# A list scheduler's DMA times, its queue limit and its table of priorities are replaced in an attention and mixture-of-experts kernel

## The chip, the cores and the metric

The kernel runs on one core of one Trainium2 chip. The metric is the device time of one execution in microseconds (us). The core has five instruction streams that run side by side and meet at semaphores: PE (matrix multiply; its weight loads are shown as PEld), DVE, ACT, POOL, and SP, which here only issues DMAs. Each stream runs strictly in the order in which the program was written.

## What is computed

Attention in two resolutions makes x, and a mixture of eight experts is applied to x. Shapes: q, k, v are 4 x 8 x 576 x 64 (batch, head, position, width), x is 2304 x 512, w1 is 8 x 512 x 1024, w2 is 8 x 1024 x 512, all float32.

```python
q_d, k_d, v_d = (z.reshape(B, H, S // 4, 4, D).mean(axis=3) for z in (q, k, v))
out_up = np.repeat(sm_attn(q_d, k_d, v_d), 4, axis=2)          # coarse attention, full softmax
mask = np.abs(pos[:, None] - pos[None, :]) < 4
out_local = softmax(where(mask, scale * q @ k.T, -1e9)) @ v    # local attention, a band of 7
x = (out_up + out_local).transpose(0, 2, 1, 3).reshape(B * S, H * D)

noisy_logits = x @ w_gate + log1p(exp(x @ w_noise)) * noise
top2 = np.argpartition(-noisy_logits, 2, axis=1)[:, :2]        # and softmax weights over the two
for e in range(8):
    for k in range(2):
        mask = top2[:, k] == e
        out[mask] += top2_w[mask, k, None] * (relu(x[mask] @ w1[e]) @ w2[e])
```

## The kernel before

**Stages.** The first part computes attention, the routing, and the first layer of expert 0. The second part (the loop over e at the end) is a fixed sequence of matrix products: for each expert the second layer (`gemm2`, tiles py, L1195) of five tiles of 126 rows, and the first layer of the next expert (`gemm1`, tiles ph, L1170). The first part has no written order: a list scheduler makes it.

**Attention.** For each batch, `t_load` brings nine blocks of q and k (tiles nat, L416 and L419), `t_pe` transposes them on PE (pt, L427), `t_copy` and `t_sum`/`t_sumq` write the transposed copies and the sums over four positions (sq and qd, on POOL and DVE). `vd_load` brings v for the coarse attention (vg, L465), `vd_sum` and `vd_sum2` add it up on POOL (vh, vd). The `d_` steps are the coarse attention: scores sd, maximum, exponential, norm pd, transpose ptd, product od, spread up. The `l_` steps are the local attention over 20 tiles of 116 positions: `l_load_v` (vw, L587), scores sc, softmax sb, transpose ptl, product o (L647), the sum `l_x` into xT. A finished chunk of 128 rows is transposed (ptx), stored to DRAM (`l_store`, x_d, L688) and multiplied with the gate weights (`l_lg` to `l_ls`, tiles pl and ps).

**Routing.** The 18 chunks form five groups of 4, 4, 4, 2 and 4. For each group, ACT and DVE find the two experts of each row, PE counts positions (`r_pos`, tiles pp, L756 to L759), DVE computes slots (sli), and POOL writes one list entry per row and choice by indirect DMAs (`r_put`, list_d, L824), 36 in all, eight for a group of four chunks. After the third group, SP loads the list of expert 0 (`a_list`, L979), and POOL gathers three tiles of x rows for it (`b_gather`, gx, L993). The other two tiles of expert 0 take their rows from a product on PE (`b_list`, pb, L788) after the last group. Gathered tiles are copied (xr), transposed (ptg, L1097) and split; then `b_gemm` computes the first layer of expert 0 in two parts, ph0a (columns of the three tiles) and ph0b (the other two), both at L1117, eight steps f each.

**Other transfers.** `fetch_w1` loads eight blocks of expert 0's w1 (raw, L189), which ACT and DVE split into a high and a low part (w0h, w0l); `fetch_w2` the same for w2 (L192, w1h, w1l). `fill_out` writes zeros to the output in six DMAs of 768 KB (out_dram<-zero, L173). `fill_list` fills the lists.

**The scheduler.** Each piece of work is a `Step` with an engine, an assumed duration, the steps it needs, the buffers it takes from rings and frees, and a priority: a number that follows its batch, tile or chunk, plus an offset for its kind from the table `OFF`. `run_steps` takes, again and again, the step that can start first by the assumed times (with `SLACK` as tolerance, ties by priority) and emits it. A step of SP has a second number, `move`, the time for which its transfer occupies the one DMA queue that the scheduler knows; `free["move"]` is when that queue is free, and a transfer counts as landed 0.9 after its move. The scheduler's clock is only used while the program is built; on the chip the order stays, the times do not.

**Fillers.** Where the scheduler expects PE to be idle, `keep_warm` puts matmuls on a tile of ones (L364), whose result nobody reads.

The calls that make the steps of the first part are in the body of `tile_attn_moe_kernel`, with `move` and the duration as arguments. Two lines of `run_steps` set what an SP step costs:

```python
free["move"] = max(x.end + 0.5, free.get("move", 0.0)) + x.move
x.done = free["move"] + 0.9
```

Of the kernel before, what the change touches and what calls it, by code (L numbers as in the profile page):

```python
# [22 lines left out]
def kernel(  # L23
# [42 lines left out]
    NA = NTA * TR  # L66
    NBC = max(256, NCOL - NA)
# [24 lines left out]
    masks = []  # L92
# [175 lines left out]
    free = {}  # L268

    def run_steps(stage):  # L270

        todo = [x for x in steps if x.end is None and x.stage <= stage]
        while not all((not x.early, x.light, False)[stage - 1] for x in todo):
# [39 lines left out]
        "a_count": 19.6, "a_holes": 29.2, "a_list": -59.7, "a_rows": -6.7, "b_gather": -36.7,  # L313
        "b_gemm": -33.7, "b_hi": -59.3, "b_list": -39.3, "b_lo": 6.8, "b_order": -53.9, "b_pe": -51.4,
        "b_relu": 19.1, "b_rest": 19.4, "b_rows": -39.1, "b_weights": -39.8, "c_count": -47.8,
        "c_fills": 6.3, "c_first": -28.0, "c_ids": 24.7, "c_masks": 32.3, "c_route": -8.3, "c_sel": 14.0,
        "c_tiles": -19.3, "d_exp": -46.9, "d_max": -48.9, "d_norm": 4.3, "d_pt": -37.6, "d_ptc": -53.4,
        "d_pv": -51.1, "d_qk": -52.0, "d_rz": -58.3, "d_up": -21.6, "fetch_w1": 13.7, "fetch_w2": 22.7,
        "fill_list": -51.7, "fill_out": 36.3, "gather": -54.0, "identb": -47.2, "init_kz": -2.2,
        "l_exp": -29.6, "l_lg": -37.8, "l_lgc": -60, "l_lgt": -58.9, "l_load_v": 9.9, "l_ls": -52.8,  # L320
        "l_max": 18.0, "l_norm": 12.6, "l_pt": 6.9, "l_ptc": -12.8, "l_pv": 21.6, "l_qk": 31.9,
        "l_store": 24.9, "l_sum": 31.1, "l_x": -5.2, "l_xt": -23.7, "l_xtc": -17.5, "list_rows": -54.6,
        "load_list": -4.8, "load_noise": -32.5, "load_wgn": 14.3, "masks": -26.6, "ones": 19.0,
        "r_count": 38.4, "r_hot": -20.5, "r_oh": 31.7, "r_pay": -59.0, "r_pos": -33.2, "r_put": 33.4,
        "r_slot": 15.0, "r_soft": 23.3, "r_top": -38.1, "r_wexp": -4.9, "r_where": -60, "split_hi1": 40,
        "split_hi2": 31.3, "split_lo1": 26.2, "split_lo2": 32.3, "t_copy": -16.9, "t_load": -38.3,
        "t_new": 20.1, "t_pe": 6.3, "t_sum": -10.2, "t_sumq": 2.4, "vd_load": -27.3, "vd_sum": 0.9,
        "vd_sum2": -46.2, "warm": -38.1}
    SLACK = 0.15
# [28 lines left out]
    pw, warm = [], []  # L358
# [26 lines left out]
    KW = 0  # L385
# [17 lines left out]
    s_wgn = [Step("load_wgn", "sp", 0.65, lambda i=i: load_wgn(i), after=[s_fills], prio=KW + 0.5 * i, move=0.3) for i in range(2)]  # L403
    s_noise = [Step("load_noise", "sp", 0.5, load_noise, prio=KO, move=0.7)]
    s_fill = Step("fill_list", "sp", 0.45, fill_list, after=[s_fills], prio=2, move=0.5)
# [440 lines left out]
    for b in range(B):  # L846
# [42 lines left out]
        for u in range(5):  # L889
# [6 lines left out]
            a1 = Step("d_qk", "pe", 0.5 if u else 0.65, lambda b=b, u=u: d_qk(b, u), cols=576 if u else 2304, after=s_sum, use=[qdb], new=scb + [pdb], prio=pc_)  # L896
# [21 lines left out]
        for i in range(NB):  # L918
# [7 lines left out]
            a1 = Step("l_qk", "pe", 1.26, lambda n=n: l_qk(n), cols=4600, after=need + [s_masks], use=[qtb, kzb[b]], new=[scb], prio=n + KQ)  # L926
# [6 lines left out]
            a8 = Step("l_pv", "pe", 1.24, lambda n=n: l_pv(n), cols=2048, after=[a7, lv], use=[pTb, vwb], new=[ob], prio=n + KP)  # L933
# [6 lines left out]
            for ck, g, c, w in ps_:  # L940
# [6 lines left out]
                s_store += [Step("l_store", "sp", 0.45, lambda n=ck: l_store(n), after=[a11], use=[xb], move=0.7, **kw)]  # L947
                a12 = Step("l_lg", "pe", 0.3, lambda n=ck: l_lg(n), cols=2048, after=[s_x, s_sel] + s_wgn, use=[xTb[ck]], new=[lgb, lsb], **kw)
# [49 lines left out]
    for g, (n0, ni) in enumerate(groups):  # L998
# [213 lines left out]
    for part in range(2):  # L1212
        w_ = (NBC if part else NA) / 2400.0
# [160 lines left out]
```

## Time and profile before

| | us |
|---|---|
| median of 3 runs (lowest, highest) | 662.92 (661.96, 671.3) |
| the profiled execution | 662.21 |
| its span, first to last instruction | 660.5 |
| PE busy | 614.6 |
| DVE, ACT, POOL busy | 348.0, 259.9, 345.3 |
| first layer of expert 0 starts on PE | 202.77 |
| second layer of expert 0 starts on PE | 231.50 |

A row of a timeline gives start and duration in us, the engine, the line, the operation with output<-input, the shapes and the count; the bracket gives the idle time of the engine ahead of it and what ended that. SPq is the instruction stream of SP. A matmul's end is modelled, so PE's busy time counts fillers and slow matmuls alike. The granted clock is the share of full speed that PE was allowed.

### The profile page before, as it was taken

The numbers are of one execution on the slowest core, as the hardware profiler recorded it, in microseconds if no ns is written. First come the engines' busy times: TensorE is split into PE (matmuls) and PEld (weight loads), VectorE is DVE, ScalarE is ACT, GpSimd is POOL, SyncE is SP. The second block draws the span as 40 slices with busy tenths as digits, with TensorE's granted clock in tenths as the row PEclk, the third lists the DMA queues.
The fourth block names the chain that finished last, engine by engine and source line by source line (L and its number), as shares of the span: only waits on it lengthen the run. The fifth ranks groups of instructions, "written<-read, shape, count | busy, mean of one in ns | idle before, by whom it ended". The sixth has DMA issues, their size and how long they took to land.

```text
span 660.5 us, 12445 instructions
## 1 busy us (share of the span) xinstructions
PE 614.6 (93%) x4710; PEld 539.1 (82%) x4710; DVE 348.0 (53%) x784; ACT 259.9 (39%) x530; POOL 345.3 (52%) x415
## 2 busy tenths in 40 slices
PE   8878697888989999999999999999999999999993
PEld 6566586666879988988998998899899889889982
DVE  5557486676966445355345435544543544453310
ACT  6658585945643332332233233233323323322200
POOL 6464334678457563746556374464656527553011
PEclk9789797979989999999999999999999999999997
DMA  9889897742355334635534463563554436455111
GB/s 170 166 185 286 200 220 173 180 117 68 108 135 99 95 106 147 176 114 169 161 111 146 131 179 107 152 174 92 170 159 139 132 115 184 123 166 142 34 45 33
DMA packets 139354, 92.66 MB, mean 140 GB/s; under 512 B 74624, under 2 KB 121216, under 8 KB 139284
## 3 DMA queue, kind: packets, MB, share of 16 engines
q1 hardware_dynamic: 126052, 62.75, 37.0%
q0 software_dynamic: 13232, 29.02, 15.5%
q8 instruction: 39, 0.64, 0.4%
q14 instruction: 31, 0.25, 0.1%
HBM read 72.66 MB, written 19.95 MB: 140 GB/s over the span
## 4 chain that ended last, share of the span: by engine, by line
PE 79%; DMA 8%; DVE 3%; POOL 3%; issue 2%; SPq 1%; ACT 1%; POOLq 0%; DVEq 0%; ACTq 0%
PE py L1195 34%; PE ph L1170 30%; PE ph0a L1117 3%; DMA nat<-in_q_dram 2%; PE sc L599 2%; PE ph0b L1117 2%; DMA nat<-in_k_dram 2%; PE pt L427 2%; DMA gx<-x_d,cl 1%; PE o L647 1%; PE ptd L540 1%; DMA raw<-in_moe_w_dram 1%; POOL list_d L824 1%; PE sd L503 1%; DMA vg<-in_v_dram 1%
## 5 line engine op out<-in xcount | busy, mean ns | idle before, releaser
L1070 POOL DMA_INDIRECT gx<-x_d,gi x140 | 143.4, 1024 | 50.3 <-issue 48.4
L1170 PE MATMUL ph<-xh,w0h 128*128 128x316 f32 x448 | 137.8, 308 | 0.0
L1170 PE MATMUL ph<-xl,w0h 128*128 128x316 f32 x448 | 137.8, 307 | 0.0
L1170 PE MATMUL ph<-xh,w0l 128*128 128x316 f32 x448 | 137.7, 307 | 0.0
L1195 PE MATMUL py<-w1l,hh 128*126 128x512 f32 x320 | 126.2, 394 | 0.0
L1195 PE MATMUL py<-w1h,hh 128*126 128x512 f32 x320 | 126.2, 394 | 0.0
L1195 PE MATMUL py<-w1h,hl 128*126 128x512 f32 x320 | 126.1, 394 | 0.0
L1205 POOL DMA_INDIRECT out_dram<-ga,lt x40 | 42.5, 1064 | 142.2 <-DVE ga L1204 90.6
L1175 DVE SCALAR_TENSOR_TENSOR hl<-ph,hh 128x632 fp32r<-128x632 f32 x56 | 45.7, 816 | 119.3 <-ACT hh L1174 119.3
L1174 ACT ACTIVATE hh<-ph 128x632 fp32r<-128x632 f32 x56 | 39.1, 698 | 152.1 <-PE ph L1170 152.1
L1170 PEld LDWEIGHTS ph<-xl,w0h 128*128 128x128 f32 x448 | 84.2, 188 | 0.3
L1170 PEld LDWEIGHTS ph<-xh,w0l 128*128 128x128 f32 x448 | 84.5, 189 | 0.0
L1170 PEld LDWEIGHTS ph<-xh,w0h 128*128 128x128 f32 x448 | 84.1, 188 | 0.3
L1195 PEld LDWEIGHTS py<-w1l,hh 128*126 128x126 f32 x320 | 59.7, 186 | 14.6
L1195 PEld LDWEIGHTS py<-w1h,hl 128*126 128x126 f32 x320 | 59.6, 186 | 14.4
L1195 PEld LDWEIGHTS py<-w1h,hh 128*126 128x126 f32 x320 | 59.6, 186 | 14.3
L1204 DVE SCALAR_TENSOR_TENSOR ga<-py,lt,ga 126x512 f32<-126x512 f32 x35 | 26.3, 751 | 69.7 <-PE py L1195 69.7
L1157 ACT ACTIVATE xh<-xr 128x504 fp32r<-128x504 f32 (+1 forms) x35 | 22.0, 628 | 104.0 <-DVE xr L1155 104.0
L1183 POOL DMA_INDIRECT ga<-out_dram,cl x35 | 36.1, 1031 | 25.2 <-DMA out_dram<-ga,lt 16.7
L824 POOL DMA_INDIRECT list_d<-pay,sli x36 | 37.3, 1037 | 21.0 <-DVE sli L803 8.6
L199 ACT ACTIVATE w0h<-raw 128x512 fp32r<-128x512 f32 x64 | 39.1, 624 | 20.8 <-DMA raw<-in_moe_w_dram 20.8
L204 DVE TENSOR_TENSOR w1l<-raw,w1h 128x512 fp32r<-128x512 f32 x64 | 43.7, 685 | 6.2 <-ACT w1h L199 6.2
(176 smaller groups left out, 958.5 us busy)
## 6 DMA issues: line engine op xcount, KB each, us to landing
raw<-in_moe_w_dram SPq DMA_DIRECT2D x128, 256.0 KB
vw<-in_v_dram SPq DMA_DIRECT2D x80, 64.0 KB
vg<-in_v_dram SPq DMA_DIRECT2D x16, 288.0 KB
out_dram<-zero SPq DMA_DIRECT2D x6, 768.0 KB
x_d<-x SPq DMA_DIRECT2D x18, 256.0 KB
nat<-in_q_dram SPq DMA_DIRECT2D x16, 256.0 KB
nat<-in_k_dram SPq DMA_DIRECT2D x16, 256.0 KB
gx<-x_d,gi POOLq DMA_INDIRECT x140, 2.9
```

What stands on the lines that cost most here:

```text
L199: nc.scalar.activation(hi, raw, AF.Copy)
L204: nc.vector.tensor_tensor(lo, raws.pop((e, z, f)), hi.bitcast(F32), op=ALU.subtract)
L824: ins = nc.gpsimd.indirect_dma_start(out=list_d[:, :], out_offset=bass.IndirectOffsetOnAxis(ap=sli[:, kk, i : i + 1], axis=0), in_=pay[:, ...
L1070: nc.gpsimd.indirect_dma_start(out=gx[:, u].rearrange("p c i -> p (c i)"), out_offset=None, in_=x_d[:, :], in_offset=bass.IndirectOffsetOn ...
L1117: nc.tensor.matmul(ph[:, 0:n], lhsT=w[:, c, :], rhs=xx[:, c, sl], start=(c == 0 and z == 0), stop=(c == NDC - 1 and z == 2))
L1170: nc.tensor.matmul(ph[:, n, 0:NH], lhsT=w[:, c, :], rhs=xx[:, c, sl], start=(c == 0 and z == 0), stop=(c == NDC - 1 and z == 2))
L1174: nc.scalar.activation(hh, ph[:, :, 0:NH], AF.Relu)
L1175: nc.vector.scalar_tensor_tensor(out=hl, in0=ph[:, :, 0:NH], scalar=0.0, in1=hh.bitcast(F32), op0=ALU.max, op1=ALU.subtract)
L1183: nc.gpsimd.indirect_dma_start(out=acc[:TR], out_offset=None, in_=out[:, :], in_offset=bass.IndirectOffsetOnAxis(ap=cl[:TR, t : t + 1], ax ...
L1195: nc.tensor.matmul(py[:TR], lhsT=hx[:, sl], rhs=w, start=(f == 0 and z == 0), stop=(f == NFC - 1 and z == 2))
L1204: nc.vector.scalar_tensor_tensor(out=acc[:TR], in0=py[:TR], scalar=wt, in1=acc[:TR], op0=ALU.mult, op1=ALU.add)
L1205: nc.gpsimd.indirect_dma_start(out=out[:, :], out_offset=bass.IndirectOffsetOnAxis(ap=lt[:TR, t, 0:1], axis=0), in_=acc[:TR], in_offset=No ...
```

## The change

`run_steps` now also limits SP: a step on SP ends no sooner than `LEAD` = 4.0 before the DMA queue is free, so issues no longer run ahead of the queue without bound, and the time at which SP is free is set after that. The `move` times of most loads and stores are larger (t_load 0.8 to 1.25, vd_load 0.9 to 1.25, fetch_w1 0.8 to 1.2, fill_out 2.3 to 2.8, noise 0.7 to 3.7), that of l_load_v smaller (1.6 to 1.3). Some assumed durations of PE steps and of `r_put` differ. All 78 offsets in `OFF` are new numbers. No operation on data is added or removed, except fillers; the order of nearly all steps of the first part is another.

```diff
             if x.table:
                 x.end += 1.28 * (x.table[0] != free.get("table", "exp"))
                 free["table"] = x.table[1]
-            free[x.eng] = x.end
             x.done = x.end + x.lag
             if x.eng == "sp":
+
+                x.end = max(x.end, free.get("move", 0.0) - LEAD)
                 free["move"] = max(x.end + 0.5, free.get("move", 0.0)) + x.move
                 x.done = free["move"] + 0.9
+            free[x.eng] = x.end
...
     OFF = {
-        "a_count": 19.6, "a_holes": 29.2, "a_list": -59.7, "a_rows": -6.7, "b_gather": -36.7,
...
+        "a_count": -30.7, "a_holes": 35, "a_list": 16.5, "a_rows": -44, "b_gather": 21.8, "b_gemm": -19,
...
-    SLACK = 0.15
+    SLACK, LEAD = 0.15, 4.0
...
-    s_noise = [Step("load_noise", "sp", 0.5, load_noise, prio=KO, move=0.7)]
-    s_fill = Step("fill_list", "sp", 0.45, fill_list, after=[s_fills], prio=2, move=0.5)
+    s_noise = [Step("load_noise", "sp", 0.5, load_noise, prio=KO, move=3.7)]
+    s_fill = Step("fill_list", "sp", 0.45, fill_list, after=[s_fills], prio=2, move=1.0)
...
-                       prio=p0 + 0.25 * (m + hh) - 2.0, move=0.8) for hh in range(2 if c < 2 else 1)]
+                       prio=p0 + 0.25 * (m + hh) - 2.0, move=1.25) for hh in range(2 if c < 2 else 1)]
...
-            lv = Step("l_load_v", "sp", 2.6, lambda n=n: l_load_v(n), new=[vwb], prio=n - KV, move=1.6)
+            lv = Step("l_load_v", "sp", 2.6, lambda n=n: l_load_v(n), new=[vwb], prio=n - KV, move=1.3)
...
-                s_put.append(Step("r_put", "pool", 1.08, lambda g=g, n0=n0, i=i, kk=kk: r_put(g, n0, i, kk), after=[b5, b6, s_fill, s_list],
+                s_put.append(Step("r_put", "pool", 1.2, lambda g=g, n0=n0, i=i, kk=kk: r_put(g, n0, i, kk), after=[b5, b6, s_fill, s_list],
...
-        a1 = Step("fetch_w1", "sp", 0.45, lambda f=f: fetch_w(0, 0, f), new=[rb], light=True, prio=8 + 1.2 * f, move=0.8)
+        a1 = Step("fetch_w1", "sp", 0.45, lambda f=f: fetch_w(0, 0, f), new=[rb], light=True, prio=8 + 1.2 * f, move=1.2)
...
-        Step("fill_out", "sp", 0.45, lambda f=f: fill_out(f), after=[s_fills], light=True, prio=FO + f, move=2.3)
+        Step("fill_out", "sp", 0.45, lambda f=f: fill_out(f), after=[s_fills], light=True, prio=FO + f, move=2.8)
```

**SP, zero fills and expert weights.** Before, these rows stand in SP's order while batch 2's q and k are being loaded (nat are q and k, vg v for the coarse attention, raw the expert's weights, out_dram<-zero the fills; lines of the new file are one higher than those of the old):

```order
L416 DMA nat_1_0_0_591<-in_k_dram 128x8x64
L189 DMA raw_595<-in_moe_w_dram 128x4x128
L189 DMA raw_629<-in_moe_w_dram 128x4x128
L465 DMA vg_0_1_632<-in_v_dram 72x4x256
L189 DMA raw_647<-in_moe_w_dram 128x4x128
L416 DMA nat_1_0_1_652<-in_k_dram 128x8x64
L173 DMA out_dram<-zero 1536x1x128
L416 DMA nat_0_1_0_679<-in_q_dram 128x8x64
L173 DMA out_dram<-zero 1536x1x128 x5
L416 DMA nat_0_1_1_804<-in_q_dram 128x8x64
```

Now the first fill stands behind the last q, k and vg load of the fourth batch, and the rest between the last local v windows (vw), x stores (x_d) and the load of expert 0's list (lt, lte):

```order
L588 DMA vw_2062<-in_v_dram 64x4x64 x4
L173 DMA out_dram<-zero 1536x1x128 x3
L588 DMA vw_2205<-in_v_dram 64x4x64 x4
...
L588 DMA vw_2746<-in_v_dram 64x4x64 x4
L980 DMA lt_120<-list_d 126x6
L980 DMA lte<-list_d 126x2x2
L173 DMA out_dram<-zero 1536x1x128
L189 DMA raw_2821<-in_moe_w_dram 128x4x128
L189 DMA raw_2837<-in_moe_w_dram 128x4x128
L689 DMA x_d<-x_2840 128x512
```

All six fills and all eight w1 loads have moved from the first half of the attention to its end; five x stores stand behind the list's load, where before two did.

**PE, from the last logits to the first layer of expert 0.** Before (ps are logits, pp positions of the last group, pb the row numbers of the last two tiles, ptg gathered tiles, o<-ones fillers):

```order
L678 MATMUL ptx_3044<-ident,xT_2964 128x128 x4
...
L704 MATMUL ps_3059<-sel,lgT_3041 128x16
L364 LDWEIGHTS ones
L364 MATMUL o_118<-ones 128x128
...
L759 MATMUL pp_3183<-m_3104,tri 128x8
...
L788 MATMUL pb<-idp,hot_0_3053 128x2
...
L1097 MATMUL ptg_3315<-ident,xr_0_3302 128x128 x4
...
L1097 MATMUL ptg_3348<-ident,xr_1_3329 128x128 x4
```

Now, from the last local product on:

```order
L648 MATMUL o_119<-pT_2946,vw_2746 64x58 x16
L1098 MATMUL ptg_3041<-ident,xr_0_3033 128x128 x4
L1098 MATMUL ptg_3049<-ident,xr_1_3039 128x128 x4
L696 MATMUL pl_3062<-xT_2950,wgn 32x128 x4
L1098 MATMUL ptg_3070<-ident,xr_2_3060 128x128 x4
L679 MATMUL ptx_3076<-ident,xT_2950 128x128 x4
L705 MATMUL ps_3087<-sel,lgT_3067 128x16
...
L1118 MATMUL ph0a_3119<-xh_2782,w0h_2651 128x378
...
L760 MATMUL pp_3185<-m_3178,tri 128x8
...
L789 MATMUL pb<-idp,hot_0_2965 128x2
```

The three gathered tiles are transposed ahead of the last logits instead of behind the last group's row numbers, and two of the eight steps of ph0a stand ahead of the last group's positions, a third ahead of pb. The fillers there (73 between ps and pp, 91 behind pp) are 17 now.

**POOL, the puts of a routing group.** Before, the second group's eight puts (sli_2145) have a normalisation (sb) between them after the sixth:

```order
L626 TENSOR_TENSOR sb_2261<-sb_2261,rz_2324 128x512
L823 MEMSET dummy 128x1
L824 DMA list_d<-pay,sli_2145 19456x2
...
L626 TENSOR_TENSOR sb_2405<-sb_2405,rz_2470 128x512
...
L824 DMA list_d<-pay,sli_2145 19456x2
L626 TENSOR_TENSOR sb_2441<-sb_2441,rz_2505 128x512
```

Now the second group's eight puts (sli_2215) stand in one block, ahead of a normalisation and of the query sums of batch 3's last block (sq, qd), which PE's coarse scores need:

```order
L627 TENSOR_TENSOR sb_1886<-sb_1886,rz_1974 128x512
L824 MEMSET dummy 128x1
L825 DMA list_d<-pay,sli_2215 19456x2
...
L627 TENSOR_TENSOR sb_2026<-sb_2026,rz_2256 128x512
L455 TENSOR_TENSOR sq_2_0_2475<-qT_1026 128x128
L456 TENSOR_TENSOR qd_1027<-sq_2_0_2475 128x4x16
L824 MEMSET dummy 128x1
L825 DMA list_d<-pay,sli_2482 19456x2
```

The third group's puts (sli_2482) follow at once; behind its eighth stand the three gathers of expert 0.

More of the change, by code (lines that the diff above doesn't have):

```diff
@@ new lines @@
+        "d_up": -33.1, "fetch_w1": 31.7, "fetch_w2": -40.1, "fill_list": 29.3, "fill_out": 26.5,
+        "gather": 21.2, "identb": -46.9, "init_kz": -33, "l_exp": 10.1, "l_lg": 14.3, "l_lgc": 14.8,
+        "l_lgt": -47.1, "l_load_v": -8.3, "l_ls": -19.6, "l_max": 29.3, "l_norm": 33.4, "l_pt": 34.1,
+        "l_ptc": -16.5, "l_pv": 18.3, "l_qk": 7.3, "l_store": -39.1, "l_sum": 35.1, "l_x": -0.4,
+        "l_xt": 14.6, "l_xtc": -0.5, "list_rows": -18.1, "load_list": -47.8, "load_noise": 27.1,
+        "load_wgn": -24.2, "masks": -39.9, "ones": -27.2, "r_count": 38.3, "r_hot": -16.8, "r_oh": -60,
@@ L402 @@
     s_sel = Step("c_sel", "dve", 0.15, c_sel, after=[s_first, s_fills], prio=KW)
-    s_wgn = [Step("load_wgn", "sp", 0.65, lambda i=i: load_wgn(i), after=[s_fills], prio=KW + 0.5 * i, move=0.3) for i in range(2)]
-    s_noise = [Step("load_noise", "sp", 0.5, load_noise, prio=KO, move=0.7)]
-    s_fill = Step("fill_list", "sp", 0.45, fill_list, after=[s_fills], prio=2, move=0.5)
+    s_wgn = [Step("load_wgn", "sp", 0.65, lambda i=i: load_wgn(i), after=[s_fills], prio=KW + 0.5 * i, move=0.7) for i in range(2)]
+    s_noise = [Step("load_noise", "sp", 0.5, load_noise, prio=KO, move=3.7)]
+    s_fill = Step("fill_list", "sp", 0.45, fill_list, after=[s_fills], prio=2, move=1.0)
     st = {}
@@ L880 @@
                 vg = buf("vg")
-                l_ = Step("vd_load", "sp", 0.45, lambda b=b, c=c, hh=hh: vd_load(b, c, hh), new=[vg], prio=pc_ - 1.0, move=0.9)
+                l_ = Step("vd_load", "sp", 0.45, lambda b=b, c=c, hh=hh: vd_load(b, c, hh), new=[vg], prio=pc_ - 1.0, move=1.25)
                 vhb = buf("vh")
@@ L895 @@
                 s_c = []
-            a1 = Step("d_qk", "pe", 0.5 if u else 0.65, lambda b=b, u=u: d_qk(b, u), cols=576 if u else 2304, after=s_sum, use=[qdb], new=scb + [pdb], prio=pc_)
+            a1 = Step("d_qk", "pe", 0.45 if u else 0.5, lambda b=b, u=u: d_qk(b, u), cols=576 if u else 2304, after=s_sum, use=[qdb], new=scb + [pdb], prio=pc_)
             a2 = Step("d_max", "dve", 0.39 if u else 0.45, lambda b=b, u=u: d_max(b, u), after=[a1] + d_0, use=scb + [zdb],
@@ L922 @@
             obs[n] = ob
-            lv = Step("l_load_v", "sp", 2.6, lambda n=n: l_load_v(n), new=[vwb], prio=n - KV, move=1.6)
+            lv = Step("l_load_v", "sp", 2.6, lambda n=n: l_load_v(n), new=[vwb], prio=n - KV, move=1.3)
             need = [x_ for (bb, z, c, hh, zz, j), x_ in s_t.items()
                     if bb == b and P * (2 * c + hh) < start(i) + TB + 10]
-            a1 = Step("l_qk", "pe", 1.26, lambda n=n: l_qk(n), cols=4600, after=need + [s_masks], use=[qtb, kzb[b]], new=[scb], prio=n + KQ)
+            a1 = Step("l_qk", "pe", 1.35, lambda n=n: l_qk(n), cols=4600, after=need + [s_masks], use=[qtb, kzb[b]], new=[scb], prio=n + KQ)
             a2 = Step("l_max", "dve", 1.35, lambda n=n: l_max(n), after=[a1], use=[scb], new=[sbb], prio=n + KQ)
@@ L932 @@
             a7 = Step("l_ptc", "act", 0.48, lambda n=n: l_ptc(n), after=[a6], use=[ptb, pTb], prio=n + KS)
-            a8 = Step("l_pv", "pe", 1.24, lambda n=n: l_pv(n), cols=2048, after=[a7, lv], use=[pTb, vwb], new=[ob], prio=n + KP)
+            a8 = Step("l_pv", "pe", 1.1, lambda n=n: l_pv(n), cols=2048, after=[a7, lv], use=[pTb, vwb], new=[ob], prio=n + KP)
             ps_ = pieces(n)
@@ L946 @@
                 a11 = Step("l_xtc", "act", 0.49, lambda n=ck: l_xtc(n), after=[a10], use=[ptxb], new=[xb], **kw)
-                s_store += [Step("l_store", "sp", 0.45, lambda n=ck: l_store(n), after=[a11], use=[xb], move=0.7, **kw)]
-                a12 = Step("l_lg", "pe", 0.3, lambda n=ck: l_lg(n), cols=2048, after=[s_x, s_sel] + s_wgn, use=[xTb[ck]], new=[lgb, lsb], **kw)
+                s_store += [Step("l_store", "sp", 0.45, lambda n=ck: l_store(n), after=[a11], use=[xb], move=1.0, **kw)]
+                a12 = Step("l_lg", "pe", 0.35, lambda n=ck: l_lg(n), cols=2048, after=[s_x, s_sel] + s_wgn, use=[xTb[ck]], new=[lgb, lsb], **kw)
                 a12 = Step("l_lgt", "act", 0.18, lambda n=ck: l_lgt(n), after=[a12], use=[lgb, lsb], **kw)
@@ L1212 @@
     for part in range(2):
-        w_ = (NBC if part else NA) / 2400.0
+        w_ = (NBC if part else NA) / 2200.0
         sg = 3 if part else 2
@@ L1238 @@
         rb = buf("raw")
-        a1 = Step("fetch_w2", "sp", 0.45, lambda f=f: fetch_w(0, 1, f), new=[rb], prio=31 + f, move=0.8, stage=3)
+        a1 = Step("fetch_w2", "sp", 0.45, lambda f=f: fetch_w(0, 1, f), new=[rb], prio=31 + f, move=1.0, stage=3)
         a2 = Step("split_hi2", "act", 0.52, lambda f=f: split_hi(0, 1, f), after=[a1], use=[rb], prio=45 + f, stage=3)
```

23 lines of the change are left out of this document (8 added, 15 removed).

## The prediction

> **What bounds the kernel now.** I read the page first, then the busy time by stage, then the chain of waits, then the waits of PE itself. The profiled execution took 662.21 us, 1.7 more than its span and 0.7 less than the median of the runs (662.92); the sum is made against it.
>
> ```profile
> span 660.5 us, 12445 instructions
> PEclk9789797979989999999999999999999999999997
> DMA  9889897742355334635534463563554436455111
> ```
>
> Each digit stands for 16.5 us. The clock granted to PE dips, and the DMA engines are full, in the first third only. The stages below are cut at four events: the positions of the third routing group (170.33, from here on called T3), the last logits (185.65, called L), the first matmul of expert 0 (202.77), and the first matmul of its second layer (231.50, called Q). The columns are length, then busy time of PE, PEld, DVE, ACT and POOL, the granted clock, the DMA share and GB/s.
>
> ```profile
> 0.00:170.33 170.33, 138.71 (x1746) 110.66 (x1747) 113.35 (x317) 111.32 (x274) 95.27 (x156) 0.91 0.77 175
> 170.33:185.65 15.32, 15.16 (x261) 12.67 (x258) 13.84 (x60) 9.27 (x20) 9.16 (x16) 1.00 0.30 82
> 185.65:202.77 17.12, 13.91 (x209) 13.26 (x209) 11.09 (x62) 7.20 (x12) 10.77 (x16) 0.90 0.59 155
> 202.77:231.50 28.73, 28.73 (x200) 28.70 (x198) 14.52 (x32) 9.97 (x22) 16.95 (x23) 1.00 0.45 93
> ```
>
> From 202.77 to Q PE never rests, and from Q on both programs hold the same code. So the change can act only on Q. The chain of waits (start, us, what) shows the part before Q that is pure matmul:
>
> ```profile
> 202.96 2.13 PE ph0a L1117 x12
> 205.53 14.61 PE ph0a L1117 x84
> 220.14 11.36 PE ph0b L1117 x96
> ```
>
> One step of ph0a (12 matmuls) takes 2.1 us, all of ph0b 11.4.
>
> **The front, up to T3.** PE waits there longest in four places; the bracket is the idle time before the row, and what ended it:
>
> ```profile
> 39.29 1.09 PE L427 MATMUL pt<-ident,nat 128*128 128x128 f32 x4 [3.08 <-DMA nat<-in_k_dram]
> 74.81 1.09 PE L427 MATMUL pt<-ident,nat 128*128 128x128 f32 x4 [5.15 <-DMA nat<-in_q_dram]
> 107.17 2.57 PE L647 MATMUL o<-pT,vw 64*64 64x58 f32 x32 [2.84 <-DMA vw<-in_v_dram]
> 134.08 0.68 PE L496 MATMUL sd<-qd 64*32 64x144 f32 x16 [4.61 <-POOL qd L455]
> ```
>
> Together 15.7 us. The second has its cause in the DMA queue: the first row below is SP issuing five of the six zero fills, the second (from the chain) the q load issued behind them.
>
> ```profile
> 54.34 11.46 SPq L173 DMA_DIRECT2D out_dram<-zero  x5
> ```
> ```profile
> 65.92 8.76 DMA nat<-in_q_dram
> ```
>
> The new order issues no fill and no expert weight before the last q, k and pooled-v load of the fourth batch, so this wait goes. It brings batch 1's q and k ahead of all local v windows, which aims at the first wait. At each of the four places the clock is at half rate directly around or behind the wait:
>
> ```profile
> 38.60:42.00 3.40, 2.71 (x18) 2.55 (x19) 0.96 (x2) 1.32 (x4) 3.16 (x6) 0.51 0.92 199
> 72.70:79.50 6.80, 4.69 (x26) 3.28 (x26) 1.12 (x2) 0.79 (x2) 3.97 (x6) 0.51 0.67 158
> 106.90:113.70 6.80, 6.54 (x67) 4.95 (x67) 2.11 (x10) 0.89 (x3) 2.84 (x6) 0.50 0.82 200
> 134.20:141.00 6.80, 6.80 (x102) 5.97 (x100) 5.42 (x18) 2.50 (x13) 4.40 (x8) 0.50 0.54 123
> ```
>
> PE was busy 20.7 us in them at a clock of 0.5, so at full clock the same work takes 10.4 us less. The Trainium skill (TensorE: Matmul & The Clock Gate, section "HAM oscillation — how this bites in real kernels") puts the threshold at idle gaps of more than about 3.4 us. By that rule only the gaps of 5.15 and 4.61 us cost clock, (4.69 + 6.80) / 2 = 5.7 us; the rows show half rate behind the 3.08 and 2.84 us gaps too, so I keep 10.4. By the rule the forecast would be 2.3 us higher.
>
> So 15.7 + 10.4 = 26.1 us can go. How much does go is not to be read from before: behind each late load stands the next thing, a POOL sum, a DVE maximum, an ACT copy, and all of PE, DVE and ACT are busy 111 to 139 us of 170. The bounds are 0 and 26.1; I take the half, 13.0, because two of the four waits (the q load behind the fills, the k load of batch 1) have a direct cause in the order of SP that is removed, and the other two (a v window, and a POOL sum) stand in chains that the new order still has.
>
> **Work that moves behind T3.** Against before, PE's order puts these behind the third group's positions: two tiles of local P·V, the whole coarse attention of batch 3 (five softmax transposes, four P·V, the score products), three gather transposes, and five small steps that I leave out. Their prices, from the groups of PE lines in 0:231.5 (busy us, mean ns):
>
> ```profile
> L647 PE MATMUL o<-pT,vw 64*64 64x58 f32 x640 | 25.9, 233 | 3.0 <-DMA vw<-in_v_dram 2.8
> L540 PE MATMUL ptd<-ident,pd 128*72 128x128 f32 x80 | 11.1, 283 | 1.0 <-DVE pd L533 1.0
> L562 PE MATMUL od<-pts,vd 72*64 72x144 f32 x128 | 9.4, 292 | 0.1
> L503 PE MATMUL sd<-qd 64*128 64x144 f32 x64 | 8.8, 348 | 0.3 <-ACT up L570 0.3
> ```
>
> 25.9 / 20 x 2 = 2.6, 11.1 / 20 x 5 = 2.8, 9.4 / 16 x 4 = 2.4, 8.8 / 4 = 2.2: 10.0 us less ahead of T3. New T3 = 170.3 - 10.0 - 13.0 = 147.3.
>
> **From T3 to the last logits.** The three gather transposes now stand ahead of the last logits in PE's order, so L waits for the list of expert 0. Before, that chain ran like this on POOL and DVE (the DVE rows are the list arriving, and the first gathered tile being copied):
>
> ```profile
> 145.23 1.46 POOL L533 TENSOR_TENSOR pd<-pd,rzd 128x288 f32<-128x288 f32 x2
> ...
> 172.93 1.01 POOL L824 DMA_INDIRECT list_d<-pay,sli  x1 [8.57 <-DVE sli L803]
> ...
> 182.34 0.97 POOL L824 DMA_INDIRECT list_d<-pay,sli  x1 [0.19 <-issue]
> ...
> 190.81 1.01 POOL L993 DMA_INDIRECT gx<-x_d,cl  x1 [0.30 <-issue]
> ```
> ```profile
> 188.13 0.16 DVE L990 SCALAR_TENSOR_TENSOR cl<-lt 126x3 int32<-126x3 int32 x1 [1.34 <-DMA lt<-list_d]
> ...
> 195.87 0.43 DVE L1090 COPY xr<-gx 128x512 f32<-128x512 f32 x1 [1.79 <-DMA gx<-x_d,cl]
> ```
>
> From T3 to the first put 2.6; eight puts 10.4 (172.93 to 183.31, one each 1.3); two norms that POOL now has between them 1.5; last put to list 4.8; row numbers and issue 0.5 (an estimate); third gather 2 x 1.3 later, data 5.1 after its issue, 7.7; copy 0.4, transpose, store transpose and logits 1.5 (estimates from steps of 0.3 to 0.6 us). Sum 29.4. PE's own work in that stretch is shorter, at most 15.2 + 10.0 + 1.8 = 27.0, and the 15.2 of before hold fillers. So the chain sets L = T3 + 29.4, and some us of PE idleness appear here that before has after L. On SP the last five x stores stand behind the load of this list; three x buffers cover two or three of them, and what is held is the same chain, so I add nothing (0 to 5).
>
> **From the last logits to Q.** Before, 45.85 us: the routing of the last group, its list, and five gathers stand alone, with fillers (first row) on PE.
>
> ```profile
> 185.65 4.24 PE L364 MATMUL o<-ones 128*128 128x128 bf16 x73
> 191.52 0.17 PE L759 MATMUL pp<-m,tri 128*128 128x8 bf16 x1 [1.62 <-DVE m L743]
> 194.88 0.51 PE L788 MATMUL pb<-idp,hot 128*128 128x2 bf16 x12
> ```
>
> Now: logits to positions 5.9 (two ph0a steps, 4.2, run in it); positions to the row numbers of tiles 3 and 4, 3.4 + 0.5 (one ph0a step inside); then three steps 6.3, which end 10.2 after the positions. The last gather is issued about 2.3 after the row numbers, its data come 5.1 later, copy and transpose take 1.0: 12.3. Two more steps 4.2, ph0b 11.4: 27.9. Q = L + 5.9 + 27.9 = L + 33.8, which is 12.0 less than before.
>
> **What could take it back.** The list of expert 1 is read after the 36th put; DVE computes its rows, then POOL gathers:
>
> ```profile
> 210.62 1.35 POOL L824 DMA_INDIRECT list_d<-pay,sli  x1 [0.19 <-issue]
> ...
> 219.87 0.99 POOL L1070 DMA_INDIRECT gx<-x_d,gi  x1 [7.89 <-issue]
> ```
>
> From the end of the last put (211.97) to the first gather of expert 1 7.9 us. In the new order eight puts (10.4) follow the last gather of expert 0 (7.2 after the positions), so that gather starts 7.2 + 10.4 + 7.9 = 25.5 after the positions, 2.4 us ahead of Q; before it was 11.6 ahead. DVE's queue has the row numbers ahead of the last five remainders of ph0b, and those free ph0b's three buffers: an estimated 0.3 us. Expert 1's five tiles must be there 27.9 us after Q; twenty gathers and two scatters at 1.3 us are 28.6, so the fifth tile comes some 2 us late, but only for the second half of the columns. I take 0, and keep 2.5 for the range.
>
> Three fills stand on SP directly ahead of the v window of tile 14, which PE needs right ahead of T3. 11.46 / 5 = 2.3 us of issue each; the load behind five of them landed 8.76 us after its issue. Three windows are buffered and PE has four tiles of work between; I take 0, and keep 8.8.
>
> The other three fills and the expert weights now share the DMA engines with puts and gathers. In 170.33:185.65 the DMA share was 0.30, so there is room. The Trainium skill (DMA: Bandwidth & Descriptors, section "Issuing engines are not separate DMA queues") says that transfers of all issuing engines run on the same 16 DMA engines and interleave, which speaks against this move: by it a gather beside a fill would take up to one fill longer, 2.3 us, and the forecast would be 643.5 on the profile's scale. I keep the row's 5.1, since that gather ran beside weight loads too.
>
> Fillers: PE's order holds 327 before and 174 after. Before L the two counts are nearly equal; those that go stood behind it, where matmuls now fill most of the time. They cost nothing where PE had nothing to do.
>
> **Sum.** Q = 147.3 + 29.4 + 33.8 = 210.5 against 231.5: 21.0 less, 662.2 - 21.0 = 641.2, and 0.7 more on the scale of the median: 642.
>
> **The rivals.** (1) All the waits and the lost clock go: 13.1 us less, 628. For it: the DMA share of 0.77 ahead of T3 holds six fills and eight weight loads, and only three fills stay there. Against it: loads were not all that PE waited for (PE idled 31.6 us there, 15.7 in the four rows). (2) None goes, since each place only uncovers the next wait: 13.0 more, 655, the gain of the tail alone. For it: rows such as the POOL sum at 134.08. (3) Slower: POOL bounds the front. Its order puts five puts of the first routing group, and eight of the second, in one block each ahead of a normalisation and of the query sums that PE waits for. 13 x 1.3 = 16.9 us on PE's path, each gap followed by half rate like those above, 2 x 3.4 = 6.8, and nothing of the 13.0 gained: 642 + 36.7 = 679. It decides against the kernel once the blocks and what does not go in the front add up to over 21 us. Against it: POOL was busy 95 of 170 us there, and before has blocks of puts too. That the change leaves the order as it was is excluded by the rows of the order.
>
> **Numbers.** About 2% (13 us) is what a measurement of this kernel tells from no change: faster is below 650, slower above 676. Forecast (634 to 649) 0.48, rival 1 0.14, rival 2 0.23 (650 to 660, a sixth of it below 650), rival 3 0.12, and 0.03 for a time like before. Faster 0.48 + 0.14 + 0.04 = 0.66; slower 0.12 and a little for the costs kept for the range together, 0.13; within 2% the remaining 0.21. The range takes in rival 1 and rival 2 with the costs of 2.5 and 2.3 us: 627 to 660; its own part for the likeliest case is 634 to 649.
>
> **What would show it.** Right: the second layer of expert 0 (py, L1196 in the new file) starts near 210; the third group's positions near 147; no wait of PE for a q, k or v load over 2 us after the first 30 us; the gather transposes ahead of the last logits, with PE idle some us there in wait for the gather; ph of expert 1 27.9 us after the first py. Wrong: PE waits for the P·V of tile 14 with the DMA named, or for sb and qd with POOL and list_d named (rival 3); T3 near 160 with new waits of 3 us and half rate behind them (rival 2); a gap ahead of expert 1.

## The result, and the profile after

The changed kernel takes 636.17 us (median of 5, 634.34 to 642.57) against 662.92 before. The ratio is 0.959, 95% interval 0.951 to 0.967. A second set, shown below as the run "after_again", gives 0.962 (0.955 to 0.969). The forecast was 642, range 627 to 660.

The page of the changed kernel, the rows that answer to those of before:

```profile
span 640.8 us, 12132 instructions
PEclk9999799879998999999999999999999999999998
DMA  9979887767756364544535545463553536345011
```

The profiled execution took 642.57 us, the slowest of the five. The dips of the clock at the left are fewer, and the DMA engines are as full as before.

Busy time by stage, cut at the same events: T3, L (the first filler behind the last logits, as at 185.65 before), Q. Columns: length, then PE, PEld, DVE, ACT, POOL, granted clock, DMA share, GB/s.

```profile
0.00:139.32 139.32, 123.13 (x1581) 100.87 (x1582) 105.95 (x292) 99.64 (x232) 91.28 (x154) 0.94 0.87 173
139.32:174.50 35.18, 29.18 (x430) 23.72 (x430) 24.89 (x90) 22.42 (x60) 17.94 (x28) 0.94 0.77 211
174.50:211.14 36.64, 32.99 (x248) 31.96 (x246) 24.57 (x88) 17.20 (x35) 14.58 (x22) 0.95 0.55 120
211.14:640.80 429.66, 418.51 (x2306) 373.95 (x2304) 195.05 (x315) 122.07 (x204) 220.88 (x212) 0.99 0.45 132
```

T3 comes 31.0 us earlier (170.33 to 139.32), T3 to L takes 19.9 more (15.3 to 35.2), L to Q 9.2 less (45.9 to 36.6), and behind Q nothing changed but 0.7 us. In the first stage PE's idle time went from 31.6 to 16.2 us and its busy time from 138.7 to 123.1.

The three largest waits of PE in the whole stretch up to T3 (what waited, for whom, us in total, times, the longest):

```profile
PE o L648 <- DMA vw<-in_v_dram: 4.8, 6, 1.6
PE pp L760 <- DVE m L744: 4.4, 2, 2.3
PE ptd L541 <- DVE pd L534: 4.2, 6, 1.6
```

None of the four waits that the prediction counted is left. What is left are small waits, six of them on v windows.

### The profile page after: what moved, and what is told of

Read it like the earlier page. It is cut to its first block, busy times and chain, and to the rows that moved or that the text cites. A ratio compares the mean times of both kernels' runs of the same rounds, so it can differ in the third digit from the quotient of the medians.

```text
span 640.8 us, 12132 instructions
## 1 busy us (share of the span) xinstructions
PE 603.8 (94%) x4557; PEld 530.5 (83%) x4557; DVE 350.5 (55%) x784; ACT 261.3 (41%) x530; POOL 344.7 (54%) x415
## 4 chain that ended last, share of the span: by engine, by line
PE 61%; DMA 1%; POOL 1%; DVE 0%; issue 0%; ACT 0%; POOLq 0%; DVEq 0%
PE py L1196 30%; PE ph L1171 30%; DMA gx<-x_d,gi 1%; POOL gx L1071 0%; DMA out_dram<-ga,lt 0%; DVE ga L1205 0%; POOL out_dram L1206 0%; DVE xr L1156 0%; DVE xl L1159 0%; ACT xh L1158 0%; POOLq L1304 0%; DVEq L1156 0%
## 5 line engine op out<-in xcount | busy, mean ns | idle before, releaser
L1184 POOL DMA_INDIRECT ga<-out_dram,cl x35 | 36.6, 1045 | 26.8 <-DMA out_dram<-ga,lt 18.2
L825 POOL DMA_INDIRECT list_d<-pay,sli x36 | 36.9, 1025 | 16.6 <-issue 5.7
```

The source lines that it names most:

```text
L825: ins = nc.gpsimd.indirect_dma_start(out=list_d[:, :], out_offset=bass.IndirectOffsetOnAxis(ap=sli[:, kk, i : i + 1], axis=0), in_=pay[:, ...
L1184: nc.gpsimd.indirect_dma_start(out=acc[:TR], out_offset=None, in_=out[:, :], in_offset=bass.IndirectOffsetOnAxis(ap=cl[:TR, t : t + 1], ax ...
```

## The experiments

**The changed kernel once more (after_again).** No edit.

> The changed kernel once more, for a second profile and for the spread between executions. Theory: the positions of the third routing group (T3) are again near 139, the last logits (L) near 172, the first py of expert 0 (Q) near 211, and the time is 634 to 643 us. Rival: the 8 us between the fastest and the slowest of its five timings come from one wait that falls differently, and Q is then several us earlier in a fast execution.

635.19 us (634.64 to 638.57). Its stages:

```profile
0.00:134.36 134.36, 120.40 (x1582) 98.53 (x1583) 105.52 (x288) 97.84 (x227) 90.52 (x151) 0.94 0.87 180
134.36:169.05 34.69, 28.84 (x427) 23.26 (x427) 26.03 (x96) 24.09 (x65) 19.13 (x31) 0.95 0.79 212
169.05:203.64 34.59, 31.68 (x248) 30.63 (x246) 24.67 (x88) 17.19 (x35) 13.11 (x21) 1.00 0.53 125
```

The same program, Q 7.5 us earlier: 5.0 of it are there at T3, 0.5 more at L, 2.0 come in the tail. This execution shows none of the waits on v windows (4.8 us in the first). So, as far as two profiles tell, much of the spread between executions is in loads that come just in time, and the term T3 has to be read from both: 134 to 139. The rival, that one wait makes the spread, has the earlier Q right, but the waits are several small ones.

In this expectation and the later ones "the last logits" is the last product with the gate weights (pl, 172.35 in the first profile), some 2.2 us ahead of L; where an expected stretch is compared, it is counted so.

**The new table alone.** The kernel before with the table of the changed one (87 offsets, every one different):

```diff
     OFF = {
-        "a_count": 19.6, "a_holes": 29.2, ...
+        "a_count": -30.7, "a_holes": 35, ...
```

> The kernel before with the new table of priorities and nothing else: its old transfer times, no queue limit. Theory 1 (the new order is the table's, the model only fits its times): 634 to 648 us. Theory 2 (the table holds only with the model it was worked out for; without the limit the list lets SP run ahead and orders PE, DVE and POOL by loads that come later): 655 us or more, with PE waits on loads of over 3 us in the first 140 us.

659.71 us, ratio 1.000 (0.998 to 1.003): no gain at all, and theory 2 holds. The longest wait of PE up to T3 (164.75):

```profile
53.31 1.12 PE L631 MATMUL ptl<-ident,sb 128*128 128x128 f32 x4 [4.54 <-POOL sb L625]
```

That is a wait of the kind of rival 3, PE for a sum that stands on POOL behind other work. The table's order for POOL is good or bad only together with the order of the loads.

**The limit alone, and the new times alone.** The kernel before with the queue's limit; and the changed kernel with the old table and no limit:

```diff
-            free[x.eng] = x.end
             x.done = x.end + x.lag
             if x.eng == "sp":
+                x.end = max(x.end, free.get("move", 0.0) - LEAD)
...
+            free[x.eng] = x.end
...
-    SLACK = 0.15
+    SLACK, LEAD = 0.15, 4.0
```
```diff
     OFF = {
-        "a_count": -30.7, "a_holes": 35, ...
+        "a_count": 19.6, "a_holes": 29.2, ...
-    SLACK, LEAD = 0.15, 4.0
+    SLACK, LEAD = 0.15, 1e9
```

> The kernel before, in which the list schedule is given the DMA queue's limit (a lead of 4 us) and nothing else: old transfer times, old table. Theory 1 (the limit is what puts loads in the right order): 640 to 652 us. Theory 2 (a table holds only with the model that it was worked out for, as the new table alone gave 659.7): 656 us or more.

> The changed kernel with the old table and without the limit, so the new transfer times and step times alone. Theory 1 (the times alone order the loads better): 640 to 652 us. Theory 2 (old priorities are offsets to old times): 656 us or more, with waits of PE of over 3 us in the front.

658.59 us, ratio 0.995 (0.992 to 0.997), and 659.78 us, ratio 0.995 (0.992 to 0.999). Both gain half a per cent at the median; theory 2 holds for both times. Its sign for the new times, waits of PE of over 3 us, does not show: the longest up to T3 is 2.1. The limit alone takes waits away and makes others:

```profile
73.09 1.71 PE L563 MATMUL od<-pts,vd 72*64 72x144 f32 x12 [4.45 <-POOL vd L482]
119.94 2.16 PE L428 MATMUL pt<-ident,nat 128*128 128x128 f32 x8 [6.82 <-DMA nat<-in_k_dram]
```

Limit and new times together with the old table give no order (the list comes to a point where no step can run), so that pair has no time. Each of the three parts alone is worth 0.0 to 0.5%, the whole 4%. The new table with only one of the other two was not run, so which of them it needs is open.

**The fills late in the kernel before.** Only the six zero fills move, on SP's queue; every other row of every engine stays. The list schedule runs as it is, but a fill is put into the queue ahead of a step that is named.

```diff
+    fills_ahead = {("l_load_v", 14): (0, 1, 2), ("l_store", 15): (3, 4, 5)}
...
-            x.fn()
+            if x.kind == "fill_out":
+                held_fills.append(x.fn)
+            else:
+                for f_ in fills_ahead.get((x.kind,) + tuple(x.fn.__defaults__ or ()), ()):
+                    fill_out(f_)
+                x.fn()
```

> The kernel before, in which only the six zero fills move on SP's queue: three ahead of the v window of tile 14, three behind the x store of tile 15; every other row of every engine as before. Theory 1 (the fills ahead of the q load were a cause of the front's loss): the wait of 5.15 us at 74.8 and the half rate behind it go, 3 to 8 us less, 655 to 660 us. Theory 2 (each place only uncovers the next wait): 661 to 665 us, with a new wait of 3 us or more within the next 20 us.

651.82 us, ratio 0.988 (0.980 to 0.996): 8.1 us less, theory 1, and more than its 3 to 8 us. (The last three fills stand ahead of the x store of tile 15, not behind it.) The wait of 5.15 us at 74.8 is gone, and the granted clock is 1.00 from 60 to 84 us. T3 is 153.12 in its profile (of an execution of 647.40 us), 17 us earlier than before, but not all of it lasts. The ninth put on POOL, which comes behind the list load, waits 9.0 us (6.1 before; the bracket names an x store, which SP issues right behind that load), and the list load goes out 6.2 us after the eighth put (3.3 before): three fills now stand beside these puts. (The edits of a run shift its line numbers by up to 8.)

```profile
165.09 0.97 POOL L832 DMA_INDIRECT list_d<-pay,sli  x1 [0.19 <-issue]
175.19 0.97 POOL L832 DMA_INDIRECT list_d<-pay,sli  x1 [9.02 <-DMA x_d<-x]
```

**The fills early in the changed kernel.** The reverse: only the fills go back.

```diff
+    fills_ahead = {("t_load", 2, 0, 1, 0): (0,), ("t_load", 2, 0, 1, 1): (1, 2, 3, 4, 5)}
```

> The changed kernel, in which only the six zero fills move on SP's queue, back to where the kernel before has them: one ahead of the third q load and five ahead of the fourth q load of batch 2; every other row as in the changed kernel. Theory 1 (the place of the fills is a main term of the front): about 14 us of issue go ahead of the loads behind, the v windows and grouped v tiles are only just in time there, T3 comes 8 to 14 us later and the time is 644 to 652 us. Theory 2 (the new order has loads so far ahead that it hides them): within 3 us of the changed kernel on the same chip.

645.37 us, ratio 0.975 (0.968 to 0.981): 9 to 10 us more than the changed kernel, theory 1. One wait is as long as what T3 loses:

```profile
76.35 2.34 PE L656 MATMUL o<-pT,vw 64*64 64x58 f32 x32 [16.14 <-DMA vw<-in_v_dram]
```

T3 is 153.8, 14 to 19 us later (8 to 14 were expected), in the profile of an execution of 650.13 us. That is more than the whole loses: T3 to L takes 30.7 us here, not 35. In the changed kernel the fills are paid for a second time behind T3. The next rows show where (last put of the third group, first gather of expert 0, on POOL; first of the changed kernel, then of this one):

```profile
153.04 0.98 POOL L825 DMA_INDIRECT list_d<-pay,sli  x1 [0.18 <-issue]
...
163.82 1.01 POOL L994 DMA_INDIRECT gx<-x_d,cl  x1 [9.80 <-DVE cle L991]
```
```profile
169.39 0.98 POOL L833 DMA_INDIRECT list_d<-pay,sli  x1 [0.19 <-issue]
...
175.39 1.00 POOL L1002 DMA_INDIRECT gx<-x_d,cl  x1 [5.02 <-DVE cle L999]
```

9.8 us from the end of the put to the gather with fills beside the puts (8.65 in the second profile), 5.0 without. The other runs bear it out: 9.3 to 10.2 in the three below that leave the fills where the changed kernel has them, 5.0 to 6.4 in the three that take them away from the puts. SP's queue of the changed kernel around it:

```profile
149.20 1.51 SPq L173 DMA_DIRECT2D out_dram<-zero  x1
150.75 2.40 SPq L189 DMA_DIRECT2D raw<-in_moe_w_dram  x1
153.25 6.69 SPq L588 DMA_DIRECT2D vw<-in_v_dram  x8
160.27 0.37 SPq L980 DMA_DIRECT2D lt<-list_d  x1
```

Two causes are possible: the load of the list stands behind eight v window loads, or the puts themselves land late.

**The list load on POOL.** To tell these apart, the load goes to the queue that issues the puts:

```diff
-        ins = nc.sync.dma_start(out=lt[:TR], ...)
+        ins = (nc.sync if t0 and lt is not lte else nc.gpsimd).dma_start(out=lt[:TR], ...)
```

> The changed kernel, in which the two loads of expert 0's list are issued by POOL, right behind the last put of the third routing group, and not by SP behind eight v window loads; nothing else moves. Theory 1 (SP's queue, not the puts, sets when the list comes): the gathers of expert 0 start about 3 to 4 us earlier, from T3 to the last logits 29 to 30 us in place of 32.4 to 33.0, and the time is 3 us less than the changed kernel, some 632 us. Theory 2 (PE is late there anyway, with its own work and the x chain): T3 to L 32 us as before, time within 2 us of 636.

637.79 us, ratio 0.960 (0.954 to 0.966); theory 1 falls. From the put to the gather it is still 9.9 us, and T3 to the last logits is 36.4 (29 to 30 were expected). The load is issued no earlier, 7.5 us behind the last put against 6.3 and 4.9 from SP in the two profiles, since POOL now waits for the puts themselves:

```profile
147.58 1.30 POOL L825 DMA_INDIRECT list_d<-pay,sli  x1 [0.19 <-issue]
156.34 0.60 POOL L980 DMA_DIRECT2D lt<-list_d  x1 [7.46 <-DMA list_d<-pay,sli]
```

The puts land 7.5 us after the last of them left POOL. So SP's queue is not the only cause: with it out of the way the list comes no sooner. The transfers beside the puts hold it up, but which of them is not taken apart. The fills also hold back SP: in the changed kernel its eight window loads are issued from 153.25 to 159.94, while the last put goes out and behind it, so window loads move while the puts should land, and SP hardly waits for the puts ahead of the list load (0.2 us in the second profile). In the run with all fills at the end, below, SP issues the window loads earlier, and then has to wait for the puts (2.6 us):

```profile
142.50 6.22 SPq L596 DMA_DIRECT2D vw<-in_v_dram  x8
151.51 0.36 SPq L988 DMA_DIRECT2D lt<-list_d  x1
```

There the last put ends at 149.82, and the load can go 1.7 us later. Late windows alone can make the stretch long: with the limit alone no fill is issued behind 113 us, eight window loads go out from 171.39 to 177.89 around the last put, and put to gather takes 9.6 us.

**All fills at the end.** All six ahead of the x store of tile 15, behind the list load:

```diff
+    fills_ahead = {("l_store", 15): (0, 1, 2, 3, 4, 5)}
```

> The changed kernel, in which all six zero fills stand on SP ahead of the x store of tile 15, behind the last v window and the first list load; every other row as it is. Theory 1 (fills cost wherever they stand among loads that are waited for): T3 stays at 133 to 136 without a wait of PE on the v windows of tile 14, and T3 to the last logits shrinks to 29 to 31; but the x stores of the last tiles and the expert weights come some 14 us later, so the stretch from L to Q grows from 37 to 45 us or more: 636 to 644 us. Theory 2 (the DMA engines have room there): 630 to 634 us.

640.02 us, ratio 0.963 (0.954 to 0.971). T3 133.3, last put to gather 5.0 us, T3 to the last logits 30.2 (to L 32.3): the front as theory 1 has it. Then it pays: L to Q takes 45.8 us. SP issues the fills from 155.14 to 173.54, and the gather of the last two tiles waits for the x stores behind them:

```profile
181.58 0.99 POOL L1002 DMA_INDIRECT gx<-x_d,cl  x1 [15.39 <-DMA x_d<-x]
...
188.19 1.97 PE L1106 MATMUL ptg<-ident,xr 128*128 128x128 f32 x8 [8.06 <-DVE xr L1099]
```

**Four weight buffers, and no puts of the last group.** Two edits at the other wait, in the tail. There PE waited, with the clock at 0.65 in the 3.4 us around it (204.0 to 207.4), for a remainder that DVE does behind the split of a weight, and the weight was late (PE, DVE and ACT rows of the changed kernel):

```profile
205.49 0.58 PE L1118 MATMUL ph0b<-xh,w0h 128*128 128x256 f32 x1 [2.54 <-DVE hl L1132]
...
204.41 0.69 DVE L204 TENSOR_TENSOR w1l<-raw,w1h 128x512 fp32r<-128x512 f32 x1 [3.25 <-ACT w1h L199]
...
203.74 0.63 ACT L199 ACTIVATE w1h<-raw 128x512 fp32r<-128x512 f32 x1 [4.51 <-DMA raw<-in_moe_w_dram]
```
```diff
-    stage = ctx.enter_context(tc.tile_pool(name="stage", bufs=3))
+    stage = ctx.enter_context(tc.tile_pool(name="stage", bufs=4))
```
```diff
-            x.fn()
+            if x.kind != "r_put" or x.fn.__defaults__[0] < 4:
+                x.fn()
```

> The changed kernel with four buffers for raw expert weights in place of three; the order of every engine as it is. Theory 1 (the weight loads of the tail wait for a free buffer): SP issues each load one split earlier, the wait of 1.6 to 2.5 us of ph0b on the DVE remainder goes, Q is 2 to 4 us earlier, some 633 us. Theory 2 (the loads are late because the puts of the last group keep the DMA engines busy): they are issued earlier and land as late, time within 2 us of 636.

> The changed kernel without the eight puts of the last routing group (its 512 tokens are missing from the lists of the experts 1 to 7, and of expert 0 where it is read from the list); nothing else is left out. Theory 1 (the puts keep the DMA engines busy while the weights are loaded, and their split stands ahead of the remainders that free ph0b's buffers): the stretch from the positions of the last group to Q shrinks from 29.4 to 31.4 us to 27 to 28, and the weight loads between 185 and 200 us land at over 200 GB/s. Theory 2 (the tail's loss over the forecast is the order on DVE and PE, not the puts): that stretch stays above 29 us.

635.57 us, ratio 0.957 (0.951 to 0.963), and 632.98 us, ratio 0.953 (0.947 to 0.959). In both the stretch from the last group's positions to Q shrinks, to 26.9 and 26.4 us from 31.4 and 29.4, as theory 1 of each has it. With four buffers the wait on the remainder is 0.2 us, and without the puts there is none. So for this wait either is enough. The other sign of theory 1 for the puts does not show: between 185 and 200 us the DMA engines move 173 GB/s without them, not over 200.

How much the puts hold back the weight loads varies. The next rows are the 5 us from 10.75 us behind the last group's positions: the second profile of the changed kernel, then the runs without the puts, with four buffers, and with the list load on POOL. Only the second has no puts there:

```profile
185.00:190.00 5.00, 4.97 (x31) 4.97 (x32) 3.89 (x7) 2.42 (x5) 4.23 (x9) 1.00 0.53 47
```
```profile
192.00:197.00 5.00, 5.00 (x34) 5.00 (x33) 4.17 (x9) 3.35 (x7) 0.00 (x0) 1.00 0.52 157
```
```profile
190.70:195.70 5.00, 5.00 (x34) 5.00 (x33) 4.22 (x9) 2.94 (x7) 4.38 (x8) 1.00 0.63 135
```
```profile
188.10:193.10 5.00, 5.00 (x34) 5.00 (x33) 3.08 (x6) 2.15 (x5) 4.24 (x9) 1.00 0.61 150
```

At the same share of busy engines 47 GB/s move with the puts and 157 without them, but two other runs move 135 and 150 beside the same puts. Neither time can be told from the changed kernel's. In the profile with four buffers the gain of the tail is offset by T3 to L (36.9), in the one without the puts by the same stretch (40.6); these profiles are of executions of 638.06 and 637.67 us.

**Fills in other places, with four buffers.** Two arrangements without a fill beside the third group's puts:

```diff
+    fills_ahead = {("l_store", 3): (0,), ("l_store", 4): (1,), ("vd_load", 3, 0, 0): (2,), ("l_store", 5): (3,), ("l_load_v", 14): (4, 5)}
```
```diff
+    fills_ahead = {("l_store", 3): (0,), ("l_store", 4): (1, 2), ("l_load_v", 14): (3, 4, 5)}
```

> The changed kernel with two edits: four buffers for raw expert weights, and the six zero fills spread on SP so that none stands beside the puts of the third routing group: one each ahead of the x stores of tiles 3, 4 and 5, one ahead of the first grouped v load of batch 3, two ahead of the v window of tile 14. Theory 1 (beside the fills the last put takes 9 to 10 us until the first gather of expert 0, without them 5): that stretch is near 5 us, T3 to the last logits 29 to 30, positions to Q near 27, and with T3 at 134 to 136 the time is 627 to 632 us. Theory 2 (a fill costs its 2.3 us wherever it stands, now at the v windows of the front): T3 comes at 140 or later and the time stays at 634 to 640 us.

> The changed kernel with four buffers for raw expert weights and the fills in SP's gaps: one ahead of the x store of tile 3, two ahead of that of tile 4, three ahead of the v window of tile 14 as now; none beside the puts of the third group. Theory 1 (a fill is free only where neither the queue nor a load behind it is waited for; the fills at 97 and 104 us cost the front, those at 69 and 82 did not): T3 at 134 to 137, the last put to the first gather 5 us, T3 to the last logits 30, positions to Q 27 to 28, so Q near 200 and 629 to 632 us. Theory 2 (a fill costs about what it takes wherever it stands): T3 at 139 or later and 634 to 638 us.

636.28 us (631.96 to 639.39; a fifth execution took 1153 us and is left out), ratio 0.959 (0.955 to 0.963), and 634.15 us (632.68 to 638.35), ratio 0.959 (0.954 to 0.964). Both times are in the range of theory 2. The stretch behind T3 comes near to theory 1: put to gather 5.0 and 6.4 us, T3 to the last logits 30.3 and 29.3, positions to Q 28.3 and 27.0. T3 is 139.5 and 140.0, as theory 2 said; but the first profile of the changed kernel has 139.3 too, so one profile of each does not show that the fills cost this. In the first there is a wait that would account for it; in the second the longest wait of PE on a v window is 1.1 us:

```profile
107.82 2.37 PE L656 MATMUL o<-pT,vw 64*64 64x58 f32 x32 [3.55 <-DMA vw<-in_v_dram]
```

Neither beats the changed kernel beyond what can be measured. In the five arrangements of the same six fills (two of them with four buffers) the time is 634 to 645 us. An estimated 14 us of transfer (six fills at the 2.3 us that each of five took on SP before) stand beside other transfers wherever they are put; the place of before, ahead of loads that PE needs next, is the dearest.

## Why the prediction was right

**The sum was right, and its terms were not.** Q was forecast at 210.5 and came at 211.1 in the first profile (203.6 in the second). By term, forecast first, then the two profiles: T3 147.3 | 139.3, 134.4. T3 to L 29.4 | 35.2, 34.7. Last logits to the last positions 5.9 | 5.2, 5.2. Positions to Q 27.9 | 31.4, 29.4. In the first profile the errors are -8.0, +5.8, -0.7, +3.5, which add up to +0.6. The 641.2 us on the profile's scale against 642.57 is luck to that extent; against the median the forecast is 6 us high, which is the second profile's balance (-12.9, +5.3, -0.7, +1.5 = -6.8).

**The front: the step that failed is "I take the half, 13.0".** After the 10.0 us of moved work, 21.0 and 26.0 of the 26.1 us went. The moved work itself was as counted. The two waits with a cause on SP went, as argued; the other two, "in chains that the new order still has", went too. New waits did come, as rival 2 has it, but short ones: the longest up to T3 is 2.3 us. The fills out of the front's queue are a large part: at T3 they alone are worth 17.2 us in the kernel before and 14 to 19 in the changed one (single profiles), of which 8.1 and 9 to 10 us are left in the whole time. What the eight weights and the order of the other loads give is not taken apart: the table, the times and the limit do next to nothing one by one.

**The clock.** I kept 10.4 us of lost clock, and the trace bears out that short gaps cost clock. In the changed kernel no single gap of PE is over 2.6 us after the first row, and still:

```profile
61.20:64.60 3.40, 3.40 (x44) 2.57 (x45) 1.65 (x5) 0.50 (x2) 1.68 (x2) 0.57 1.05 136
64.60:68.00 3.40, 3.40 (x28) 2.96 (x26) 1.23 (x4) 1.72 (x4) 1.24 (x2) 0.50 0.97 228
119.00:122.40 3.40, 3.12 (x59) 3.09 (x60) 2.61 (x8) 1.36 (x3) 2.62 (x6) 0.60 0.37 81
```

The first two follow waits of 1.06 and 0.26 us (at 60.29 and 61.07), the last one of 2.31 (at 119.28). The Trainium skill (TensorE: Matmul & The Clock Gate, section "HAM oscillation — how this bites in real kernels") has gaps of more than about 3.4 us; these are shorter, and the measurement decides. Not every such gap costs clock: behind one of 2.04 us at 79.67 the granted clock stays at 1.00 (79.6 to 86.4).

**T3 to L: the step that failed is "last put to list 4.8".** With the 0.5 us behind it, 5.3 against 8.7 to 9.8. Of the 5.8 us that the stretch is over the forecast in the first profile 4.5 are here, and 3.4 of 5.3 in the second; another 1.1 and 1.5 come between the first gather and L. The prediction had the mechanism and turned it down: "I keep the row's 5.1, since that gather ran beside weight loads too", and "so there is room", from a DMA share of 0.30; the share is now 0.77. The Trainium skill (DMA: Bandwidth & Descriptors, section "Issuing engines are not separate DMA queues") says that the transfers of all issuing engines interleave on the same DMA engines. The trace agrees: two fills go out between the first and the last of the eight puts (at 146.35, not quoted, and 149.20; the puts run from 141.76 to 154.02), and the stretch is 3.4 to 4.5 us longer than forecast, where the prediction's estimate was up to 2.3 for one fill. Without fills there it is 5.0 (fills early, fills last). It is the list that is late, not the gather, for which I had applied it. Whether the fills do it themselves, or the window loads that they push behind the puts, stays open.

**The stores behind the list load on SP.** Kept at 0, and no cost shows: with the fills back in the front, T3 to L is 30.7, 1.3 over the forecast, and the excess stands ahead of the first put (4.5 us from T3 for 2.6).

**L to Q.** Logits to positions 5.2 for 5.9, two ph0a steps in it, as forecast. The step that failed is the price of "those free ph0b's three buffers: an estimated 0.3 us". The row numbers ahead of the remainders are not what was late; the split of an expert weight was, and it cost 2.54 us and half rate in one profile, 1.60 in the other. It goes with four buffers or without the puts.

**What could take it back.** The three fills ahead of the v window of tile 14: 0 taken, 8.8 kept; 2.6 us of waits (0.51, 0.49, 1.61) in one profile, none in the other. Expert 1's tiles: 0 taken; its first matmul comes 27.87 us after Q in both profiles, so right. Fillers: 327 to 174 without a cost to be seen.

**The rivals.** Rival 1 (all waits go, 628 on the profile's scale, 629 on the median's) is what T3 of the second profile shows, and the stretches behind T3 gave 6 us back. Rival 2 (none goes) is out. Rival 3 (POOL) does not decide here: no wait of PE on POOL is left up to T3 in the first profile, and one of 0.3 us in the second. The new table under the old model shows that it could: 4.54 us at 53.31, and no gain.

**Signs named ahead.** py near 210: yes, 211.1 and 203.6. T3 near 147: no, earlier. No wait over 2 us on a q, k or v load: yes in both (1.6 the longest). Gather transposes ahead of the last logits with PE idle: yes, 2.3 and 1.5 us of such waits. No gap ahead of expert 1: yes.

## What to carry to other kernels

A sum that comes out right says little of its terms: compare the cut points one by one, and take two profiles, since loads that come just in time can move a whole stage by 5 us between executions, as they did here. Bulk transfers that nobody waits for cost time here wherever they stood; move them away from loads that the bound engine needs, and then look at what small transfers now stand beside them, such as indirect writes. A table of priorities belongs to the cost model that it was worked out with: here the table alone gave nothing, and the model's parts alone half a per cent at most.

## What was not expected of the hardware

Small indirect writes landed late here when bulk moved beside them. With the list load on POOL the puts land 7.5 us after the last of them left POOL, where two fills and eight window loads stand beside them (the DMA engines 0.86 busy at 200 GB/s from 148.88 to 156.34); with the fills at the end the load that waits for them goes out after 1.7 us.

And busy DMA engines did not always move much: beside the last group's puts 47 GB/s at a share of 0.53, without them 157 at 0.52. The puts' own queue has only 0.7% of the engines' time in that window, that of the weight loads 52.0%. Why the weight loads are slow there, and pass at 135 and 150 GB/s beside the same puts in two other runs, no run here shows.
